# Keys of a head pair split once and carried over by DMAs, with 10 plain float32 heads instead of 12

## The chip, the cores and the metric

One core of one Trainium2 chip. The metric is the device time of one execution in microseconds (us), the median of several runs. A profiled execution has a time of its own, which is named where it is used.

## The reference

Three layers follow one another on 4 batches of 448 rows and 768 columns, all float32. The first is attention with 12 heads of 64 columns, where a sigmoid stands in place of a softmax:

```python
scores = scale * np.matmul(q, k.transpose(0, 1, 3, 2)) - np.log(S)
attn = 1.0 / (1.0 + np.exp(-scores))
return np.matmul(attn, v).astype(np.float32)
```

The second mixes each row with the row before it by two learned vectors (`mu_k`, `mu_r`), and computes sigmoid(xr @ w_r) * (relu(xk @ w_k)^2 @ w_v). The third is a mixer: a token part, u = x + relu(xt @ w_tok1) @ w_tok2, and a channel part, u + relu(u @ w_ch1) @ w_ch2. The matrices of weights arrive as float64 and are narrowed in the kernel.

## The kernel before, in words

Products of float32 accuracy are made from the fast type float32r. `split` (line 97) rounds an operand to float32r (the high part, a cast on ScalarE or VectorE, by the table of line 38) and subtracts that from the operand (the low part, always VectorE). A product then takes the high parts and the cross terms as separate matmuls.

Attention works by pairs of heads, six pairs a batch. `unit_k` (line 161) splits the keys of one head. The scores contract over 64 columns only, so the tile K has the high part of a head's keys in the half of the partitions that is the head's own, and the low part in the other half, and one matmul takes both. The keys of a pair arrive as one tile `kn`, head 0 in partitions 0 to 63 and head 1 in 64 to 127; two such tiles are held, and once both heads are split, `load_k` fetches the pair two further on. `unit_q` (line 172) splits the queries, doubled over both halves of the partitions, and the values. `unit_qk` (line 191) makes half of the scores of a head, takes the sigmoid on ScalarE, and rounds and subtracts again (lines 211 to 218). `unit_av` (line 221) multiplies with the values.

A head in the set `NATIVE` (line 51) is plain in its second product: neither its values nor its sigmoids are split, and `unit_av` makes 4 plain float32 matmuls (line 230), of which the trace records two passes each, and one copy out of PSUM. Any other head takes 7 float32r matmuls (lines 235 and 237), a copy of one half of the result on ScalarE (line 239) and an add on VectorE (line 240). Of batch 0, heads 1 to 7 and 11 are plain; of batch 1, heads 1, 4, 8 and 9; of batches 2 and 3 none.

`attention_units` (line 242) writes these units in one order. For batch 0 they run at the start, with the two mixings of each pair's columns behind it; after unit number `TOK2` the token weights are loaded and narrowed, and after number `EARLY` the first chunk of weights is made ready. The attention of each later batch is spread evenly over the matmuls of the batch before (lines 594 and 609 to 615). `first_part` (line 431) makes the second layer and the token part of one batch, `second_part` (line 532) the channel part of two batches. The weights come in chunks. At their first use a chunk is loaded as 768 KB of float64 into one of two `raw` tiles, narrowed by ScalarE and VectorE (line 268), stored as float32 for later use, and split; later uses load the stored copy.

SP issues every DMA, in order. A scheduler turns the written order into one order for each engine's queue; each queue then runs in that order and waits on semaphores. The temporaries of the pool `tmps` have four buffers of one tag, shared by the mixings and the second layer.

Of the kernel before, what the change touches and what calls it, by code (L numbers as in the profile page):

```python
# [9 lines left out]
F32 = mybir.dt.float32  # L10
F32R = mybir.dt.float32r
U32 = mybir.dt.uint32
BF16 = mybir.dt.bfloat16
# [4 lines left out]
B, H, S, D = 4, 12, 448, 64  # L18
# [4 lines left out]
P = 128  # L23
NT = C // P
NPAIR = H // 2
# [8 lines left out]
def f32(ap):  # L34
    return ap.bitcast(F32)


ONDVE = [('K', 0), ('K', 1), ('K', 2), ('K', 3), ('Q', 0), ('Q', 2), ('Q', 3), ('V', 1), ('V', 2), ('kk', 0), ('kk', 3), ('mix', 1), ('mix', 2), ('mix', 3), ('prev', 2), ('sq', 2)]

# [2 lines left out]
END_1 = 1.0  # L42
BEG_2 = 0.15
END_2 = 0.65
EARLY = 20
TOK2 = 20

NATIVE = {(0, 1), (0, 7), (0, 4), (1, 1), (0, 3), (1, 8), (1, 4), (0, 6), (0, 2), (0, 5), (1, 9), (0, 11)}


def native(b, pr, h):
    return (b, 2 * pr + h) in NATIVE


@with_exitstack
def kernel(
# [21 lines left out]
    PE, ACT, DVE, POOL, SP = nc.tensor, nc.scalar, nc.vector, nc.gpsimd, nc.sync  # L81

    def pool(name, bufs, **kw):
        return ctx.enter_context(tc.tile_pool(name=name, bufs=bufs, **kw))

    const, big = pool("const", 1), pool("big", 1)
    wraw, wpool, wsplit = pool("wraw", 2), pool("wpool", 2), pool("wsplit", 3)
    dram = pool("dram", 1, space=bass.MemoryType.DRAM)
    tmps = pool("tmps", 4)
    a1, a2, a3 = pool("a1", 1), pool("a2", 2), pool("a3", 3)  # L90
    ps_mm = pool("ps_mm", 3, space=PSUM)
    ps_av, ps_sc = pool("ps_av", 1, space=PSUM), pool("ps_sc", 2, space=PSUM)

    def ENG(kind, b):
        return DVE if (kind, b) in ONDVE else ACT

    def split(hi, lo, src, engine):
        if engine is ACT:
            ACT.copy(hi, src)  # L99
        else:  # L100
            DVE.tensor_copy(hi, src)
        DVE.tensor_tensor(out=lo, in0=src, in1=f32(hi), op=ALU.subtract)  # L102
# [4 lines left out]
    kns, qns, vns = {}, {}, {}  # L107

    def load_k(g):
        if g < B * NPAIR:  # L110
            kns[g] = a2.tile([P, 4 * P], F32, tag="kn", name="kn")
            SP.dma_start(out=kns[g], in_=k[g])

    def load_q(g):
        if g < B * H:
            qns[g] = a3.tile([P, S], F32, tag="qn", name="qn")
            SP.dma_start(out=qns[g], in_=q[g])

    def load_v(g):
        if g < B * NPAIR:  # L120
            vns[g] = a2.tile([P, 2, 4, D], F32, tag="vn", name="vn")
            SP.dma_start(out=vns[g], in_=v[g])
# [3 lines left out]
    DVE.memset(warm, 0.0)  # L126
    ACT.activation(warm, warm, AF.Sigmoid)

    zero = const.tile([P, S], BF16, tag="zero", name="zero")
    POOL.memset(zero, 0.0)  # L130
    idle = ps_av.tile([P, 512], F32, tag="av", name="idle")
    for _ in range(WARM):
# [25 lines left out]

    att = {}

    def unit_k(b, pr, h):
        g = b * NPAIR + pr
        kn = kns[g]
        me = slice(h * D, h * D + D)
        ot = slice(D - h * D, P - h * D)
        K = a3.tile([P, 4 * P], F32R, tag="KK", name="KK")
        split(K[me], K[ot], kn[me], ENG("K", b))
        att[(b, pr, h)] = {"K": K}
        if h == 1:
            load_k(g + 2)  # L170

    def unit_q(b, pr, h):
        g = b * NPAIR + pr
        st = att[(b, pr, h)]
        qn = qns.pop(2 * g + h)
        Q1 = a2.tile([P, S], F32R, tag="Q1", name="Q1")
        Q2 = a2.tile([P, S], F32R, tag="Q2", name="Q2")
        split(Q1, Q2, qn, ENG("Q", b))
        st["Q"] = (Q1, Q2)
        load_q(2 * g + h + 3)  # L180
        vn = vns[g][:, h]
        if native(b, pr, h):
            st["v"] = vn
        else:
            vs = a3.tile([P, 4, 2 * D], F32R, tag="vs", name="vs")
            split(vs[:, :, 0:D], vs[:, :, D:], vn, ENG("V", b))
            st["v"] = vs
        if h == 1:
            load_v(g + 2)

    def unit_qk(b, pr, h, c2):
        st = att[(b, pr, h)]
        K, (Q1, Q2) = st["K"], st["Q"]
        ps = ps_sc.tile([P, 2, 512], F32, tag="sc", name="psc")
        for j in range(2):
            c = c2 * 2 + j
            PE.matmul(ps[:, j, :S], K[:, c * P : (c + 1) * P], Q1, start=True, stop=False)  # L197
            PE.matmul(ps[:, j, :S], K[:, c * P : (c + 1) * P], Q2, start=False, stop=True)  # L198
        plain = native(b, pr, h)
# [21 lines left out]
    def unit_av(b, pr, h):  # L221
        st = att.pop((b, pr, h))
        vs = st["v"]
        ps = ps_av.tile([P, 512], F32, tag="av", name="pav")
        me = slice(h * D, h * D + D)
        ot = slice(D - h * D, P - h * D)
        if native(b, pr, h):
            for c in range(4):
                n = P if c < 3 else TAIL
                PE.matmul(ps[:D, :S], vs[:n, c], st[c // 2][:n, c % 2], start=(c == 0), stop=(c == 3))  # L230
            ACT.copy(xe[me, pr, 1:], ps[:D, :S])
            return
        for c in range(4):
            ah, al = st[c // 2]
            PE.matmul(ps[:, :S], vs[:, c], ah[:, c % 2], start=(c == 0), stop=(c == 3))  # L235
            if c < 3:
                PE.matmul(ps[:, :S], vs[:, c], al[:, c % 2], start=False, stop=False)  # L237
        tmp = a1.tile([P, S], F32, tag="avt", name="avt")
        ACT.copy(tmp[me], ps[ot, :S])
        DVE.tensor_tensor(out=xe[me, pr, 1:], in0=ps[me, :S], in1=tmp[me], op=ALU.add)  # L240

    def attention_units(b, then=()):

        u = [lambda: unit_k(b, 0, 0), lambda: unit_q(b, 0, 0), lambda: unit_k(b, 0, 1)]
        for pr in range(NPAIR):
            nx = pr + 1 < NPAIR
            u.append(lambda pr=pr: unit_qk(b, pr, 0, 0))
            u.append(lambda pr=pr: unit_q(b, pr, 1))
            if pr:
                u.append(lambda pr=pr: unit_av(b, pr - 1, 1))  # L250
                u += [f[pr - 1] for f in then]
            u.append(lambda pr=pr: unit_qk(b, pr, 0, 1))
            if nx:
                u.append(lambda pr=pr: unit_k(b, pr + 1, 0))
            u.append(lambda pr=pr: unit_qk(b, pr, 1, 0))
            u.append(lambda pr=pr: unit_av(b, pr, 0))
            if nx:
                u.append(lambda pr=pr: unit_q(b, pr + 1, 0))
                u.append(lambda pr=pr: unit_k(b, pr + 1, 1))
            u.append(lambda pr=pr: unit_qk(b, pr, 1, 1))  # L260
        u.append(lambda: unit_av(b, NPAIR - 1, 1))
        u += [f[NPAIR - 1] for f in then]
        return u
# [317 lines left out]
    for i, unit in enumerate(attention_units(0, [mix_units("r", box, 0), mix_units("k", box, 0)])):  # L581
        unit()
        if i == TOK2:
            load_tok2()
            w_raw(1)
        if i == EARLY:
            w_ready(1)
# [10 lines left out]
    rows, u = [], []  # L598
# [104 lines left out]
```

## Time and profile before

| what | value |
|---|---|
| median of 3 runs | 938.99 us (938.84 to 939.93) |
| profiled execution, its own time | 939.26 us |
| its span, first to last instruction | 937.5 us |
| TensorE busy | 925.3 us, 4472 matmuls |
| VectorE busy | 660.1 us |
| ScalarE busy | 516.7 us |
| DMA | 137.38 MB, 147 GB/s over the span |

The engines are named PE (TensorE matmul), PEld (TensorE weight load, which overlaps PE), DVE (VectorE), ACT (ScalarE), POOL (GpSimd) and SP (SyncE). Matmuls are pipelined: a record's duration reaches into the next record, so the time of a block of matmuls is read from start to start. Tensor names are the program's: `KK` are the split keys, `kn` the keys as loaded, `psc` the scores in PSUM, `pav` the product with the values, `al` and `ah` the parts of the sigmoids, `vs` the split values, `whi` and `wlo` the split weights. The granted clock of TensorE is 1.00 of full speed throughout.

### The profile page before, as it was taken

To read this page: it belongs to the slowest core of one execution; us is meant where nothing else is said; L and a number is where in the kernel's file an instruction comes from. 1 tells how busy PE (TensorE), PEld (TensorE's weight loads), DVE (VectorE), ACT (ScalarE), POOL (GpSimd) and SP (SyncE) were. 2 spreads that over 40 slices of the span, in tenths; PEclk is the share of its full clock that TensorE was granted. 3 is DMA by queue.
4 is the path that set the end of the run, shared out by engine and by line. 5 is a ranking of instruction groups with operands and counts; after the bars stand their busy time and mean duration, and the time that the engine had idled before them with its cause. 6 is when DMAs were issued, how large, how long until landed. Compare 5 with 4: busy or idle time off the path is not lost.

```text
span 937.5 us, 12121 instructions
## 1 busy us (share of the span) xinstructions
PE 925.3 (99%) x4472; PEld 804.4 (86%) x4472; DVE 660.1 (70%) x1111; ACT 516.7 (55%) x794; POOL 1.3 (0%) x10
## 2 busy tenths in 40 slices
PE   8999999999999999999999999999999999999998
PEld 4476778778998989889898999999999999898987
DVE  8999899989567898777879479988745552332231
ACT  6998989674674757555641367767444342112210
POOL 0000000000000000000000000000000000000000
PEclk9999999999999999999999999999999999999999
DMA  7637765765444456475444343323335321242132
GB/s 235 225 132 223 248 223 193 230 231 162 122 137 131 143 194 229 155 223 192 163 143 156 130 133 107 111 66 104 102 111 154 112 80 51 81 133 73 51 99 74
DMA packets 57084, 137.38 MB, mean 147 GB/s; under 512 B 6593, under 2 KB 23489, under 8 KB 57025
## 3 DMA queue, kind: packets, MB, share of 16 engines
q1 hardware_dynamic: 57024, 136.61, 45.4%
q8 instruction: 35, 0.57, 0.3%
q14 instruction: 25, 0.20, 0.1%
HBM read 106.96 MB, written 29.62 MB: 146 GB/s over the span
## 4 chain that ended last, share of the span: by engine, by line
PE 88%; DVE 6%; ACT 3%; DMA 2%; issue 1%; ACTq 0%; SPq 0%; DVEq 0%
PE psmm L415 25%; PE psmm L412 24%; PE psmm L414 24%; PE pav L230 3%; PE psc L197 3%; PE psc L198 3%; PE pav L235 2%; PE pav L237 2%; DMA raw<-in_moe_w_k_dram 2%; PE psmm L465 1%; DVE wlo L102 1%; DVE wd L278 1%; ACT a L204 1%; DVE wd L281 1%; DVE KK L102 1%
## 5 line engine op out<-in xcount | busy, mean ns | idle before, releaser
L412 PE MATMUL psmm<-Ah,whi 128*128 128x448 f32 (+2 forms) x688 | 249.1, 363 | 2.7 <-ACT whi L99 2.7
L415 PE MATMUL psmm<-Ah,wlo 128*128 128x448 f32 (+2 forms) x688 | 249.3, 362 | 0.8 <-DVE wlo L102 0.6
L99 ACT CAST whi<-wd 128x768 fp32r<-128x768 f32 (+1 forms) x160 | 121.4, 760 | 229.6 <-PE psmm L414 209.8
L414 PE MATMUL psmm<-Al,whi 128*128 128x448 f32 (+2 forms) x672 | 243.4, 362 | 0.1
L102 DVE TENSOR_TENSOR wlo<-wd,whi 128x768 fp32r<-128x768 f32 (+1 forms) x160 | 137.6, 861 | 97.6 <-ACT whi L99 96.0
L412 PE MATMUL psmm<-Mh,whi 128*128 128x448 f32 (+2 forms) x480 | 176.2, 367 | 0.1
L415 PE MATMUL psmm<-Mh,wlo 128*128 128x448 f32 (+2 forms) x480 | 175.6, 366 | 0.1
L414 PE MATMUL psmm<-Ml,whi 128*128 128x448 f32 (+2 forms) x480 | 174.7, 364 | 0.0
L412 PEld LDWEIGHTS psmm<-Ah,whi 128*128 128x128 f32 x688 | 129.1, 188 | 18.4 <-ACT whi L99 3.7
L415 PEld LDWEIGHTS psmm<-Ah,wlo 128*128 128x128 f32 x688 | 129.2, 188 | 13.7 <-DVE wlo L102 2.3
L414 PEld LDWEIGHTS psmm<-Al,whi 128*128 128x128 f32 x672 | 126.2, 188 | 11.7 <-DVE Al L102 0.6
L204 ACT ACTIVATE a<-psc 128x896 f32<-128x896 f32 x96 | 86.9, 914 | 29.8 <-PE psc L198 29.6
L415 PEld LDWEIGHTS psmm<-Mh,wlo 128*128 128x128 f32 x480 | 90.1, 188 | 11.7 <-DVE wlo L102 1.5
L412 PEld LDWEIGHTS psmm<-Mh,whi 128*128 128x128 f32 x480 | 90.2, 188 | 10.5 <-issue 0.7
L414 PEld LDWEIGHTS psmm<-Ml,whi 128*128 128x128 f32 x480 | 90.2, 188 | 8.5
L197 PE MATMUL psc<-Q,KK 128*128 128x448 f32 x192 | 71.5, 373 | 0.5 <-ACT a L204 0.4
L198 PE MATMUL psc<-Q,KK 128*128 128x448 f32 x192 | 70.3, 367 | 0.7 <-DVE Q L102 0.7
L211 ACT CAST ah<-a 128x896 fp32r<-128x896 f32 x72 | 67.7, 943 | 1.0
L273 ACT ACTIVATE wd<-raw 128x768 f32<-128x768 f32 (+2 forms) x54 | 45.1, 835 | 26.0 <-DVE wlo L102 11.4
L278 DVE SCALAR_TENSOR_TENSOR wd<-wd,raw 128x768 uint32<-128x768 uint32 (+2 forms) x54 | 47.1, 874 | 14.0 <-ACT wd L273 9.0
L235 PE MATMUL pav<-ah,vs 128*128 128x448 f32 x144 | 53.3, 370 | 0.2 <-DVE ah L218 0.2
L275 ACT ACTIVATE raw<-raw 128x768 uint32<-128x768 uint32 (+2 forms) x54 | 45.3, 838 | 9.4 <-DMA raw<-in_moe_w_ch_dram 8.4
(81 smaller groups left out, 1035.4 us busy)
## 6 DMA issues: line engine op xcount, KB each, us to landing
wd<-w SPq DMA_DIRECT2D x66, 384.0 KB, 3.1
raw<-in_moe_w_ch_dram SPq DMA_DIRECT2D x24, 768.0 KB, 4.8
w<-wd SPq DMA_DIRECT2D x38, 384.0 KB, 2.7
qn<-in_q_dram SPq DMA_DIRECT2D x48, 224.0 KB, 2.8
wd<-w SPq DMA_DIRECT2D x42, 256.0 KB, 2.7
kn<-in_k_dram SPq DMA_DIRECT2D x24, 256.0 KB, 2.7
vn<-in_v_dram SPq DMA_DIRECT2D x24, 256.0 KB, 3.2
raw<-in_moe_w_k_dram SPq DMA_DIRECT2D x8, 768.0 KB, 6.1
```

What stands on the lines that cost most here:

```text
L99: ACT.copy(hi, src)
L102: DVE.tensor_tensor(out=lo, in0=src, in1=f32(hi), op=ALU.subtract)
L197: PE.matmul(ps[:, j, :S], K[:, c * P : (c + 1) * P], Q1, start=True, stop=False)
L198: PE.matmul(ps[:, j, :S], K[:, c * P : (c + 1) * P], Q2, start=False, stop=True)
L204: ACT.activation(a, ps[:, :, :S], AF.Sigmoid, bias=-math.log(S), scale=1.0 / math.sqrt(D))
L211: ACT.copy(ah, a)
L235: PE.matmul(ps[:, :S], vs[:, c], ah[:, c % 2], start=(c == 0), stop=(c == 3))
L275: ACT.activation(lo, lo, AF.Copy, bias=0.4375, scale=0.875 * 2.0**-29)
L278: DVE.scalar_tensor_tensor(out=dst, in0=dst, scalar=3, in1=lo, op0=ALU.logical_shift_left, op1=ALU.bitwise_or)
L412: PE.matmul(ps[:, :n], wh, xh, start=(i == 0), stop=False)
L414: PE.matmul(ps[:, :n], wh, xl, start=False, stop=False)
L415: PE.matmul(ps[:, :n], wl, xh, start=False, stop=(i == count - 1))
```

## The change

The keys of a pair are now one unit, `unit_k(b, pr)`. For the first pair of a batch it splits the two heads as before, both ahead of the first query. For every other pair it rounds all 128 partitions at once into the K tile of head 1, subtracts in place in `kn`, and two DMAs carry the two halves of head 0's K: the high part from the K tile of head 1, the low part from `kn`. A third DMA, in the later unit `unit_k2`, writes head 1's low part over the half that head 0's high part has left; the load of the keys two pairs on follows it. `unit_k` stands earlier in the order of units, ahead of the other product of the pair before. Heads 1 and 11 of batch 0 leave the set of plain heads. The K tiles have four buffers instead of three; to make room, the zero tile and the copy of line 239 move to the pool `tmps`. `EARLY` and `TOK2` go from 20 to 18, one unit earlier in the new order.

```diff
-EARLY = 20
-TOK2 = 20
+EARLY = 18
+TOK2 = 18
...
-NATIVE = {(0, 1), (0, 7), (0, 4), (1, 1), (0, 3), (1, 8), (1, 4), (0, 6), (0, 2), (0, 5), (1, 9), (0, 11)}
+NATIVE = {(0, 7), (0, 4), (1, 1), (0, 3), (1, 8), (1, 4), (0, 6), (0, 2), (0, 5), (1, 9)}
...
-    a1, a2, a3 = pool("a1", 1), pool("a2", 2), pool("a3", 3)
+    a2, a3, a4 = pool("a2", 2), pool("a3", 3), pool("a4", 4)
...
-    zero = const.tile([P, S], BF16, tag="zero", name="zero")
+    zero = tmps.tile([P, S], F32, tag="tmp", name="zero").bitcast(BF16)[:, :S]
...
-    def unit_k(b, pr, h):
+    def unit_k(b, pr):
         g = b * NPAIR + pr
         kn = kns[g]
-        me = slice(h * D, h * D + D)
-        ot = slice(D - h * D, P - h * D)
-        K = a3.tile([P, 4 * P], F32R, tag="KK", name="KK")
-        split(K[me], K[ot], kn[me], ENG("K", b))
-        att[(b, pr, h)] = {"K": K}
-        if h == 1:
+        K = [a4.tile([P, 4 * P], F32R, tag="KK", name="KK") for _ in range(2)]
+        halves = [(slice(h * D, h * D + D), slice(D - h * D, P - h * D)) for h in range(2)]
+        if pr == 0:
+            for h, (me, ot) in enumerate(halves):
+                split(K[h][me], K[h][ot], kn[me], ENG("K", b))
+        else:
+
+            (me, ot), mine = halves[0], K[1]
+            split(mine, kn.bitcast(F32R), kn, ENG("K", b))
+            SP.dma_start(out=f32(K[0][me]), in_=f32(mine[me]))
+            SP.dma_start(out=f32(K[0][ot]), in_=kn[me])
+        for h in range(2):
+            att[(b, pr, h)] = {"K": K[h]}
+        if pr == 0:
             load_k(g + 2)
+
+    def unit_k2(b, pr):
+        g = b * NPAIR + pr
+        SP.dma_start(out=f32(att[(b, pr, 1)]["K"][:D]), in_=kns[g][D:])
+        load_k(g + 2)
...
-        tmp = a1.tile([P, S], F32, tag="avt", name="avt")
+        tmp = tmps.tile([P, S], F32, tag="tmp", name="avt")
...
-        u = [lambda: unit_k(b, 0, 0), lambda: unit_q(b, 0, 0), lambda: unit_k(b, 0, 1)]
+        u = [lambda: unit_k(b, 0), lambda: unit_q(b, 0, 0)]
...
             u.append(lambda pr=pr: unit_q(b, pr, 1))
+            if nx:
+                u.append(lambda pr=pr: unit_k(b, pr + 1))
             if pr:
...
-            if nx:
-                u.append(lambda pr=pr: unit_k(b, pr + 1, 0))
...
-                u.append(lambda pr=pr: unit_k(b, pr + 1, 1))
+                u.append(lambda pr=pr: unit_k2(b, pr + 1))
```

## Rows read from the trace of the kernel before

**Rows 1.** The page, busy us (share of the span) and instructions of TensorE.

```profile
PE 925.3 (99%) x4472; PEld 804.4 (86%) x4472; DVE 660.1 (70%) x1111; ACT 516.7 (55%) x794; POOL 1.3 (0%) x10
```

**Rows 2.** The waits of TensorE: who waited for whom, us, times, longest.

```profile
PE psmm L412 <- ACT whi L99: 2.7, 2, 1.5
```

**Rows 3.** Busy us of each engine by stretch (length, PE, PEld, DVE, ACT, POOL, clock, DMA).

```profile
15.00:45.00 30.00, 29.98 (x92) 13.22 (x93) 27.96 (x49) 26.55 (x41) 0.00 (x0) 1.00 0.74 237
45.00:90.00 45.00, 44.79 (x191) 32.79 (x190) 44.19 (x73) 43.55 (x66) 0.00 (x0) 1.00 0.51 159
90.00:135.00 45.00, 41.55 (x182) 32.13 (x181) 39.79 (x63) 36.64 (x55) 0.00 (x0) 1.00 0.68 233
135.00:215.00 80.00, 79.44 (x373) 64.06 (x372) 74.77 (x135) 61.84 (x104) 0.00 (x0) 1.00 0.69 227
215.00:937.50 722.50, 717.89 (x3599) 655.16 (x3597) 462.15 (x772) 339.74 (x521) 0.00 (x0) 1.00 0.40 126
```

**Rows 4.** TensorE's timeline (start, length) around a plain and a split head.

```profile
19.27 3.36 PE L230 MATMUL pav<-a,vn 128*64 128x448 f32 x8
...
22.56 0.47 PE L197 MATMUL psc<-Q,KK 128*128 128x448 f32 x1
...
301.24 0.37 PE L235 MATMUL pav<-ah,vs 128*128 128x448 f32 x1
...
302.66 0.60 PE L465 MATMUL psmm<-ident,r 128*128 128x128 f32 x4
```

**Rows 5.** Groups by shape (busy us, mean ns): what a split head adds.

```profile
L102 DVE TENSOR_TENSOR vs<-vn,vs 128x256 fp32r<-128x256 f32 x36 | 15.1, 419 | 0.5
...
L215 DVE TENSOR_TENSOR al<-a,ah 128x896 fp32r<-128x896 f32 x36 | 39.2, 1089 | 13.7 <-ACT ah L211 13.5
...
L217 DVE TENSOR_TENSOR al<-a,ah 128x448 fp32r<-128x448 f32 x36 | 22.4, 622 | 2.7 <-ACT ah L211 2.2
...
L218 DVE TENSOR_TENSOR ah<-a,ah 64x448 fp32r<-64x448 f32 x36 | 22.4, 623 | 1.0
...
L240 DVE TENSOR_TENSOR xe<-pav,avt 64x448 f32<-64x448 f32 x36 | 22.3, 621 | 6.2 <-ACT avt L239 5.6
...
L211 ACT CAST ah<-a 128x896 fp32r<-128x896 f32 x72 | 67.7, 943 | 1.0
...
L99 ACT CAST vs<-vn 128x256 fp32r<-128x256 f32 x16 | 6.4, 405 | 3.7 <-DMA vn<-in_v_dram 3.6
```

**Rows 6.** The same view: the two key steps, and a subtract of 128 partitions.

```profile
L101 DVE CAST KK<-kn 64x512 fp32r<-64x512 f32 x48 | 20.1, 418 | 3.2 <-DMA kn<-in_k_dram 2.6
...
L102 DVE TENSOR_TENSOR KK<-kn,KK 64x512 fp32r<-64x512 f32 x48 | 33.0, 686 | 1.5
...
L102 DVE TENSOR_TENSOR wlo<-wd,whi 128x512 fp32r<-128x512 f32 x56 | 38.4, 687 | 21.3 <-ACT whi L99 21.2
```

**Rows 7.** Timeline of the start: VectorE's key steps, TensorE's first reading of pair 1.

```profile
3.43 0.87 DVE L101 CAST KK<-kn 64x512 fp32r<-64x512 f32 x2 [2.57 <-DMA kn<-in_k_dram]
...
8.35 0.68 DVE L102 TENSOR_TENSOR KK<-kn,KK 64x512 fp32r<-64x512 f32 x1
...
12.90 0.37 PE L197 MATMUL psc<-Q,KK 128*128 128x448 f32 x1
```

**Rows 8.** DMA issues (KB, us to landing), and two raw loads on SP's timeline.

```profile
kn<-in_k_dram SPq DMA_DIRECT2D x24, 256.0 KB, 2.7
...
86.77 0.38 SPq L308 DMA_DIRECT2D raw<-in_moe_w_k_dram  x1
...
98.52 0.37 SPq L308 DMA_DIRECT2D raw<-in_moe_w_k_dram  x1
```

**Rows 9.** Groups by shape: weight loads of a plain and of a split head.

```profile
L235 PEld LDWEIGHTS pav<-ah,vs 128*128 128x128 f32 x144 | 27.0, 188 | 4.4 <-DVE ah L218 1.4 <-DVE xe L240 0.3
...
L230 PEld LDWEIGHTS pav<-a,vn 128*64 128x64 f32 x72 | 8.4, 136 | 14.3 <-issue 11.4 <-ACT xe L231 1.3 <-DVE xe L240 0.8
```

## The prediction

> **What bounds the kernel now.** I read the page first. TensorE is busy 925.3 of 937.5 us and its weight loads 804.4 us [rows 1]. Busy time overlaps from matmul to matmul, so the second reading is what TensorE waits for by name: the longest of these waits in the whole run, for the rounded weights of ScalarE, sums to 2.7 us [rows 2]. Third, the span cut into stretches [rows 3]. From 215 us on TensorE is busy 717.9 of 722.5 us while VectorE needs 462 and ScalarE 340: there nothing but fewer matmuls can shorten the run. Between 15 and 215 us the three engines are nearly level. From 15 to 45 us TensorE is busy 29.98 of 30, ScalarE 26.55, VectorE 27.96. From 45 to 90 us it is 44.79, 43.55 and 44.19 of 45: whoever gets more work there becomes the bound. From 90 to 135 us TensorE loses 3.45 us, the most of any stretch, while VectorE and ScalarE idle 5.2 and 8.4 us; something else is late there, the raw weights (below). So the reader should see a matmul-bound run with a fifth at the front where VectorE and ScalarE are level with TensorE, and the change works mostly in that fifth.
>
> **Two heads from plain float32 to split.** A plain head's attention times values is eight passes; one such block runs from 19.27 to 22.56 us, where the next matmul starts: 3.29 us. A split head's seven matmuls start at 301.24 us and the next kind at 302.66: 1.42 us [rows 4]. Each head moved saves TensorE 1.87 us, two save 3.7. Start to start is the price here, not the recorded duration, since records overlap. The Trainium skill (Perfetto Trace Analysis, Identifying the Most-Contended Engine) says that matmul busy time misleads and that the weight loads' busy share is to be read. On that measure eight loads of 136 ns (1.09 us) give way to seven of 188 ns (1.32 us) [rows 9], so the two heads would cost TensorE 0.5 us instead of saving 3.7. The start times of rows 4 decide for me, and the other reading is a rival below.
>
> What the two heads add [rows 5]: on VectorE the subtract of the values 0.42, the wide subtract 1.09, the two narrow ones 0.62 each and the final add 0.62, 3.37 us a head; on ScalarE two rounding copies of 0.943 and the rounding of the values 0.405, 2.29 us a head (the copy out of PSUM stands in either version). Both heads are of batch 0: VectorE +6.7 us, ScalarE +4.6 us, the first head at 10 to 20 us, the second (head 11) in the stretch of 45 to 90 us.
>
> **Keys of a pair at once.** For each pair but the first of a batch, two casts of 64 partitions (0.418 us) and two subtracts (0.686 us) become one of each over 128 partitions. A subtract of 128 x 512 takes 0.687 us [rows 6], so partitions cost nothing; the 128 x 512 cast is not in the trace, and I take the 64 x 512 one's price, with that of two as the other end. Saved: 1.10 us a pair, 5.5 us a batch, 22 us of VectorE in all; if the cast is no faster, 0.69 a pair. In batch 0 this leaves VectorE 6.7 - 5.5 = +1.2 us; in batch 1 it has 5.5 us less. The 11 us of batches 2 and 3 lie after 215 us beside a full TensorE: nothing.
>
> **What each part gives.** Head 1 sits in the stretch where TensorE alone is full. ScalarE has 3.45 us free there for 2.3 more, VectorE 2.0 us free plus 3.3 us from three pairs of keys for 3.4 more. I count the full -1.9 us (ends 0 and -1.9). Head 11 sits in the level stretch: ScalarE gets 2.3 us more and has 1.45 us free, so TensorE's 1.9 us is handed back as waits for the rounding copy. I count 0; ends -1.9 (ScalarE's work slides behind 90 us, where it idles 8.4 us) and +0.9 (2.3 - 1.45). The relief of VectorE in batch 1 can win back at most what TensorE loses from 90 to 215 us, 3.45 + 0.56 = 4.0 us [rows 3]. Most of that is late raw weights, which VectorE's relief doesn't hurry, so I take -1.0, near the end of the second stretch, with ends 0 and -4.0.
>
> **The three transfers a pair.** Each is 128 KB from SBUF to SBUF on SP's queue. No such transfer is in the trace; the nearest row is the key load, 256 KB from HBM, 2.7 us [rows 8]. Below nothing they can't go, as nobody got keys by a transfer before. The keys of pair 1 of batch 0 are subtracted at 8.35 us (done at 9.04) and first read at 12.90 [rows 7]: 3.9 us for a path that now needs 2.7 us and the issue. The change also cuts these keys earlier in the order. So 0 to 2.7 us once, and I take 0.5. The third transfer overwrites what the first reads and so waits for its landing, and behind it in SP's order wait the load of the keys two pairs on and whatever comes next, raw weights among them. In batches 1 to 3 the two-pair lead of that key load covers a late start; if it were gone, VectorE's next cast would wait 2.7 us. Moving head 1's keys ahead of the first query: both casts already run back to back at 3.43 us [rows 7], so one subtract of 0.69 us can come ahead of the query, and VectorE does the same work before the first full score; 0, ends 0 and 0.7. The copy buffer that moves into the shared temporaries, the zero tile and the earlier placing of the token weights and the first weight chunk (one unit earlier) I cost at nothing: a buffer of that pool is held for about one copy and one add, and there are four.
>
> **Sum.** -1.9 (head 1) + 0 (head 11) - 1.0 (VectorE's relief) + 0.5 (transfers) = -2.4 us against the profiled execution, 939.26 us (span 937.5 and 1.8 around it). The median, 938.99, lies 0.3 below it: 936.6 us. About 0.2%, 1.9 us, is what a measurement of this kernel tells from no change; 937.1 is the bound.
>
> **Rivals.** *TensorE is the bound throughout.* For it: busy 44.79 of 45 even in the level stretch, and only 2.7 us in its longest sum of waits. Then both heads pay in full, -3.7, and the relief gives -2.0 of its 4.0: 938.99 - 5.7 = 933.3 us. Against: ScalarE at 97% from 45 to 90 us is given 2.3 us more. Chance 0.24.
>
> *The front is bound by ScalarE and VectorE, and TensorE's saving goes.* For it: the level stretch, and VectorE's +1.2 us in batch 0. Both heads give 0, relief -1.0, transfers +0.5: 938.5 us, no change. The Trainium skill's weight-load measure above, taken alone, ends here too, +0.5 for the heads and 939.0 in all; the trace speaks against its reason and not against its result. Chance 0.22, of which the weight-load reading has 0.02.
>
> *Slower: the transfers stand in front of the raw weights.* The raw weights of the first use have two buffers; a refill of one buffer starts at 86.77 and its next at 98.52 us, 11.8 us apart [rows 8], and from 90 to 135 us this loop is what TensorE's 3.45 us are lost to. SP issues in order. If the third transfer of a pair waits for the first's landing with a raw load behind it, that load starts 2.7 us late. Three pairs of batch 1 are prepared between 77 and 135 us; with two of them in the way, +5.4 us, less the 2.4 gained, +3.0: 942.0 us, and 941.0 where the other buffer hides 1.0 us of it. It decides where SP reaches the third transfer before the first has landed. Against: that transfer is written two units later, so in most pairs the first has long landed. By the Trainium skill (SBUF — State Buffer, "Can I just issue two DMAs to hit both halves?") transfers to the two partition halves do not run side by side; the two for head 0 would then take 5.4 us, by rows 8, an estimate, and pair 1 would be 1.5 us late rather than 0.5. No row here shows a 64-partition transfer. Chance 0.19.
>
> That the change fails to do what it says I leave out: rows 6 show the price of 128 partitions outright.
>
> **How the numbers follow.** The forecast has 0.35, its own range 935 to 938: 0.29 of it faster, 0.06 within the bound. The full gain adds 0.24 to faster. The lost saving adds 0.22 to no change. The slower case gives 0.17 to slower and 0.02 to no change. Faster 0.53, same 0.30, slower 0.17. The range reaches from 932.0 (the full gain of 933.3 with another third of the 4.0 us won back; all of it would be 931.3) to 941.0 (the milder form of the slower case).
>
> **What would show it.** In the new profile TensorE has 16 plain passes fewer and 14 split matmuls more, and the blocks keep 3.29 and 1.42 us. Key subtracts number 28 instead of 48 (8 of the first pairs, 20 wide ones of about 0.69 us); VectorE falls by about 15 us in all. Right: at equal places in the matmul order TensorE is some 2 us ahead by 45 us, no further ahead at 90, a little more by 215, and unchanged after. Wrong on head 11: the lead grows between 45 and 90 us. Wrong on the transfers: TensorE's weight loads for scores wait on key transfers in batch 0, or raw loads start more than 12 us apart from 87 to 135 us. Wrong altogether if the time differs after 215 us by more than it did there.

## The result, and the profile after

The changed kernel takes 945.15 us (median of 4 runs, 943.14 to 945.51) against 939.2 us for the kernel before, run beside it: a ratio of 1.0062 with a 95% interval of 1.0048 to 1.0076. It is 5.8 us slower. The forecast was 936.6 us and faster; the time lies outside its range. The execution profiled took 944.95 us (span 943.2).

The page of the changed kernel, the lines that answer to [rows 1] (busy us, share of the span, instructions), then the end of its chain of waits:

```profile
span 943.2 us, 12216 instructions
PE 924.5 (98%) x4470; PEld 804.6 (85%) x4470; DVE 642.7 (68%) x1081; ACT 521.4 (55%) x800; POOL 1.3 (0%) x10
PE 77%; DVE 8%; DMA 8%; ACT 4%; issue 2%; SPq 0%; ACTq 0%; DVEq 0%
```

TensorE's busy time fell by only 0.8 us while the span grew by 5.7, so TensorE stands idle more. VectorE fell by 17.4 us, and the kernel is slower all the same: its busy total is not what counts. DMAs now make 8% of the chain; before they made 2% (TensorE 88, VectorE 6, ScalarE 3).

The stretches that answer to [rows 3] (length; PE, PEld, DVE, ACT, POOL busy; clock, DMA share, GB/s):

```profile
15.00:45.00 30.00, 28.11 (x90) 13.18 (x90) 26.49 (x48) 26.42 (x41) 0.00 (x0) 1.00 0.76 235
45.00:90.00 45.00, 40.88 (x177) 30.89 (x177) 42.21 (x71) 43.03 (x64) 0.00 (x0) 1.00 0.60 195
90.00:135.00 45.00, 42.87 (x187) 32.71 (x185) 38.90 (x60) 37.58 (x55) 0.00 (x0) 1.00 0.80 262
135.00:215.00 80.00, 77.31 (x362) 62.10 (x362) 71.52 (x126) 63.64 (x108) 0.00 (x0) 1.00 0.70 227
```

From 15 to 45 us TensorE lost 1.9 us of busy time, from 45 to 90 us 3.9, and there all three engines are less busy than before: TensorE 40.88, VectorE 42.21, ScalarE 43.03 of 45. No engine is full. They wait for one another, in the stretch where [rows 3] showed three level engines.

TensorE's waits of the changed kernel from 60 to 90 us (who waited for whom, us, times, longest); the kernel before has no row in this stretch:

```profile
PE psc L212 <- ACT a L219: 1.4, 1, 1.4
PE pav L250 <- DVE xe L255: 1.2, 1, 1.2
PE psmm L430 <- DVE wlo L102: 0.8, 1, 0.8
PE psmm L427 <- ACT Ah L99: 0.4, 1, 0.4
PE psmm L429 <- DVE Al L102: 0.3, 1, 0.3
```

Five short waits for five different things: scores wait for a score buffer that ScalarE's sigmoid frees, a product for the one product buffer that VectorE's add frees, the rest for mixed columns and weights. No key is among them. This is the end of batch 0, where head 11 is.

Where the lag stops is seen at equal places in the work. The last subtract of the weights of the first use, the 28th chunk (start and length of a row of two, of which it is the first), in the kernel before and then in the changed one:

```profile
200.10 1.55 DVE L102 TENSOR_TENSOR wlo<-wd,whi 128x512 fp32r<-128x512 f32 x2
```

```profile
205.77 1.55 DVE L102 TENSOR_TENSOR wlo<-wd,whi 128x512 fp32r<-128x512 f32 x2
```

It is 5.7 us late, and 5.7 us is the difference of the spans. By this mark the loss lies before 206 us. I summed TensorE's idle time against each matmul's own pitch (0.203 us from start to start for 448 split columns, 0.411 for a plain pass): the changed kernel has some 9 us more of it. Less the 3.7 that the two heads save, that gives 5 to 6 us. The largest pieces are 75 to 90 us (0.6 before, 4.3 after) and the first 30 us (about 2 more). Where the lag that stays comes in is seen by counting TensorE's matmuls from the end, so that both kernels have the same number left: the changed one is 0.9 us behind at 55 us, 2.9 at 79, 3.7 at 102, 2.5 at 127 and 5.9 at 193 in the executions profiled. So more than half of it comes in behind batch 0's attention, between 127 and 193 us. In one execution of the version without transfers told below, it grows there from 1.3 to 4.9 us too.

The price of the blocks and of the keys, in TensorE's timeline and VectorE's groups by shape, for [rows 4 and 6]:

```profile
21.50 3.36 PE L245 MATMUL pav<-a,vn 128*64 128x448 f32 x8
...
24.79 0.47 PE L212 MATMUL psc<-Q,KK 128*128 128x448 f32 x1
```

```profile
L101 DVE CAST KK<-kn 128x512 fp32r<-128x512 f32 x20 | 8.4, 421 | 0.0
...
L102 DVE TENSOR_TENSOR kn<-kn,KK 128x512 fp32r<-128x512 f32 x20 | 13.7, 686 | 0.1
...
L102 DVE TENSOR_TENSOR KK<-kn,KK 64x512 fp32r<-64x512 f32 x8 | 5.5, 687 | 0.3
```

A plain block is 3.29 us as before, and a cast of 128 partitions takes no longer than one of 64. The transfers, from the DMA issues (count, KB, median us from issue to landing), for [rows 8]:

```profile
kn<-in_k_dram SPq DMA_DIRECT2D x24, 256.0 KB, 3.0
KK<-kn SPq DMA_DIRECT2D x40, 128.0 KB, 3.6
KK<-KK SPq DMA_DIRECT2D x20, 128.0 KB, 3.4
```

By the medians, half the bytes of a key load, moved inside SBUF, land later than the load from HBM. And SP, the engine that issues nearly every load, now waits for them (SP's waits, whole run):

```profile
SPq L112 <- DMA KK<-kn: 23.2, 8, 6.2
SPq L184 <- DMA KK<-KK: 20.5, 11, 5.5
SPq L175 <- PE psc L213: 18.6, 9, 4.6
```

Line 112 is the key load two pairs on, which overwrites the tile that the last transfer reads and so waits for its landing; line 184 is the third transfer. In the first 60 us these two waits make 5.9 and 1.7 us. Raw weights stand behind them. The sixth raw load of the run, on SP's timeline before, after, and in the version with the same ten plain heads and without transfers:

```profile
39.15 0.41 SPq L308 DMA_DIRECT2D raw<-in_moe_w_r_dram  x1
```

```profile
50.55 0.42 SPq L323 DMA_DIRECT2D raw<-in_moe_w_r_dram  x1
```

```profile
50.65 0.43 SPq L321 DMA_DIRECT2D raw<-in_moe_w_r_dram  x1
```

It is 11.4 us late after the change, and as late without a single transfer. So with ten plain heads this lateness needs no transfer.

### The profile page after: what moved, and what is told of

It reads as the page before. It is cut to its first block, busy times and chain, and to the rows that moved or that the text cites. A ratio compares the mean times of both kernels' runs of the same rounds, so it can differ in the third digit from the quotient of the medians.

```text
span 943.2 us, 12216 instructions
## 1 busy us (share of the span) xinstructions
PE 924.5 (98%) x4470; PEld 804.6 (85%) x4470; DVE 642.7 (68%) x1081; ACT 521.4 (55%) x800; POOL 1.3 (0%) x10
## 4 chain that ended last, share of the span: by engine, by line
PE 77%; DVE 8%; DMA 8%; ACT 4%; issue 2%; SPq 0%; ACTq 0%; DVEq 0%
PE psmm L430 22%; PE psmm L427 22%; PE psmm L429 22%; DMA raw<-in_moe_w_ch_dram 3%; PE psc L212 3%; PE psc L213 3%; PE pav L250 2%; PE pav L252 2%; DMA raw<-in_moe_w_r_dram 1%; PE pav L245 1%; DVE wd L293 1%; DMA raw<-in_moe_w_k_dram 1%; DMA raw<-in_moe_w_v_dram 1%; DVE wd L296 1%; DVE Al L102 1%
## 5 line engine op out<-in xcount | busy, mean ns | idle before, releaser
L226 ACT CAST ah<-a 128x896 fp32r<-128x896 f32 x76 | 71.5, 943 | 1.2
L250 PE MATMUL pav<-ah,vs 128*128 128x448 f32 x152 | 56.6, 373 | 1.4 <-DVE xe L255 1.2
```

Of the source, the lines that this page charges most:

```text
L226: ACT.copy(ah, a)
```

## The experiments

Three questions: which part loses the time, what about that part costs it, and what of the two heads' saving is real. Single executions of one kernel lie mostly within 2 to 4 us of its median, one lies 7 us above it, so the verdicts go by the ratio of several runs to the kernel before on the same chip, with its 95% interval. Profiles say where.

### The parts one by one

**The change without the two heads.** The changed kernel with the 12 plain heads of before:

```diff
-NATIVE = {(0, 7), (0, 4), ..., (1, 9)}
+NATIVE = {(0, 1), (0, 7), (0, 4), ..., (1, 9), (0, 11)}
```

> The changed kernel with the 12 plain heads of before; transfers, order and buffers as changed. Theory 'heads' (the two heads' extra ScalarE and VectorE work in batch 0 costs more than TensorE's 3.7 us): back to 939 or less. Theory 'transfers' (key transfers delay keys and the DMAs behind them): 945 or more, since TensorE gets 3.7 us back on top. Theory 'order' (the new order and placing of the units): 945 or more as well.

942.1 us, 1.0032 (1.0020 to 1.0043): in none of the three ranges.

**The two heads without the rest.** The kernel before with two entries less:

```diff
-NATIVE = {(0, 1), (0, 7), (0, 4), ..., (1, 9), (0, 11)}
+NATIVE = {(0, 7), (0, 4), ..., (1, 9)}
```

> The kernel before with only the 10 plain heads. Theory 'heads': 943 to 945. Theories 'transfers' and 'order': between 935.5 (the full 3.7 us) and 939.

941.77 us, 1.0035 (1.0021 to 1.0050), where the kernel before took 938.6 beside it. So both halves lose, 0.32% and 0.35%. Together they would make about the 0.62% of the whole, but the next runs show that the parts don't simply add. The heads, which I had counted as the gain, cost 3.2 us.

**The change without the transfers.** All pairs split half by half at the new place in the order, ten plain heads:

```diff
-        if pr == 0:
+        if True:
             for h, (me, ot) in enumerate(halves):
...
-        if pr == 0:
-            load_k(g + 2)
+        load_k(g + 2)
```

> The changed kernel with every pair's keys split directly, head by head, in the changed place and order: no transfers, 22 us of VectorE work back. 10 plain heads, buffers as changed. Theory 'transfers': 935 to 939. Theory 'heads': 943 to 947. Theory 'order': 945 or so.

946.05 us, 1.0075 (1.0060 to 1.0090). With ten plain heads the transfers and the relief that they bring to VectorE together make no measurable difference: the interval overlaps that of the change.

**The earlier placing.** The changed kernel with its two placing constants at 19, half way back to 20:

```diff
-EARLY = 18
-TOK2 = 18
+EARLY = 19
+TOK2 = 19
```

> The changed kernel with EARLY and TOK2 at 19, so that the token weights and the first chunk come behind the same unit as before. If the earlier placing is the cause: 941 or less. Theories 'heads' and 'transfers': 945, within 1.5.

943.92 us, 1.0055 (1.0036 to 1.0074): not to be told from the change.

**The order alone.** The edit of the third run and the 12 plain heads: new order, new buffers, no transfers, no moved heads.

```diff
-NATIVE = {(0, 7), (0, 4), ..., (1, 9)}
+NATIVE = {(0, 1), (0, 7), (0, 4), ..., (1, 9), (0, 11)}
...
-        if pr == 0:
+        if True:
...
-        SP.dma_start(out=f32(att[(b, pr, 1)]["K"][:D]), in_=kns[g][D:])
-        load_k(g + 2)
+        pass
```

> The changed kernel with 12 plain heads and every pair's keys split directly, without transfers: what is left is the order of the units, the placing and the buffers. Theory 'order and buffers': 942 to 944. Theory 'transfers' (the 3.5 us that the changed kernel with 12 plain heads lost come from the transfers): 938 to 940.

938.63 us, 0.9995 (0.9986 to 1.0004). The new order costs nothing, so in the first run (1.0032) the transfers do, net of VectorE's relief. It also shows that the parts don't add: order alone -0.05% and heads alone +0.35%, but both together (the third run) +0.75%. That rest was not resolved.

**The buffers alone.** The kernel before with four key tiles and with the copy buffer and the zero tile in the shared temporaries.

```diff
-    zero = const.tile([P, S], BF16, tag="zero", name="zero")
+    zero = tmps.tile([P, S], F32, tag="tmp", name="zero").bitcast(BF16)[:, :S]
...
-        K = a3.tile([P, 4 * P], F32R, tag="KK", name="KK")
+        K = a4.tile([P, 4 * P], F32R, tag="KK", name="KK")
...
-        tmp = a1.tile([P, S], F32, tag="avt", name="avt")
+        tmp = tmps.tile([P, S], F32, tag="tmp", name="avt")
```

> The kernel before with the changed buffers alone: four key tiles, the copy of line 239 and the zero tile in the shared temporaries. If the shared temporaries hold up the copy or the mixings: 940.5 or more, with waits at line 239 or 399. If the order of the units is the cause: 938 to 939.5.

937.15 us, 0.9989 (0.9974 to 1.0004): nothing, as the prediction had it.

### The two heads

**One head at a time.** The kernel before, first with (0, 1) alone moved to split, then with (0, 11) alone.

```diff
-NATIVE = {(0, 1), (0, 7), (0, 4), ..., (1, 9), (0, 11)}
+NATIVE = {(0, 7), (0, 4), ..., (1, 9), (0, 11)}
```

```diff
-NATIVE = {(0, 1), (0, 7), (0, 4), ..., (1, 9), (0, 11)}
+NATIVE = {(0, 1), (0, 7), (0, 4), ..., (1, 9)}
```

> The kernel before with head 1 of batch 0 alone moved to split (11 plain heads). The ten plain heads alone measured 3.2 us over before. Theory 'start' (VectorE is full from 5.5 to 15 us, so head 1's extra work delays the start): +1.5 to +3, and head 11 little. Theory 'level stretch' (head 11's extra ScalarE and VectorE work and the two-step emptying of the one product buffer hit the stretch of 45 to 90 us): within 1 us of before, or 1 to 2 us faster.

> The kernel before with head 11 of batch 0 alone moved to split (11 plain heads). Theory 'level stretch': +1.5 to +4, with TensorE's losses rising between 60 and 90 us. Theory 'start': within 1 us of before, or up to 1.9 us faster.

1.0000 (0.9983 to 1.0017) and 1.0005 (0.9992 to 1.0018). Either head alone is free within its interval and shows no gain; together they cost 0.35%. That fits a slack that one head uses up. In the profile with both heads moved, TensorE waits in the same stretch as in the changed kernel, 60 to 90 us:

```profile
PE psmm L412 <- ACT Ah L99: 1.0, 2, 0.8
PE psc L198 <- DVE Q L102: 0.9, 1, 0.9
PE pav L235 <- DVE xe L240: 0.7, 1, 0.7
PE psc L197 <- DVE KK L102: 0.3, 1, 0.3
PE psmm L414 <- DVE Al L102: 0.3, 1, 0.3
```

These waits are not the loss by themselves. Head 11 alone loses as much to the pitch there in its profile (7.3 us; both heads 7.1, before 2.1), then loses some 4 us less than before from 90 to 135 us, and costs nothing.

**Is it ScalarE?** The prediction priced head 11 by ScalarE's free time. So in the changed kernel the rounding of batch 0's mixed columns goes from ScalarE to VectorE:

```diff
-ONDVE = [..., ('kk', 3), ('mix', 1), ...]
+ONDVE = [..., ('kk', 3), ('mix', 0), ('mix', 1), ...]
```

> The changed kernel (10 plain heads) with batch 0's rounding of the mixed columns on VectorE: 12 copies of 0.56 us leave ScalarE, 12 of 0.39 us come to VectorE. Theory 'ScalarE is the bound of the front' (the two heads' 4.6 us of ScalarE work is what costs): 939 to 942. Theory 'chains and buffers' (waits from one unit to the next, not an engine's load): 944 to 947.

951.25 us, 1.0126 (1.0109 to 1.0143). Both theories are missed, upwards. If ScalarE alone were the bound this would have helped; it cost 6 us more. VectorE has no room for it either.

**Other heads.** The changed kernel with heads 8 and 9 of batch 1 moved in place of 1 and 11 of batch 0.

```diff
-NATIVE = {..., (1, 1), (0, 3), (1, 8), (1, 4), ..., (1, 9)}
+NATIVE = {(0, 1), ..., (1, 1), (0, 3), (1, 4), ..., (0, 11)}
```

> The changed kernel with 10 plain heads, but the two that move to split are heads 8 and 9 of batch 1 instead of 1 and 11 of batch 0. Theory 'level front' (batch 0 has no room on ScalarE and VectorE, batch 1's later part has): 938 to 941, that is the 942.1 of the 12 plain heads less up to 3.7. Theory 'the plain heads cost nothing where they are' (any two heads moved lose): 944 to 946.

943.29 us, 1.0046 (1.0029 to 1.0062), against 1.0032 for the changed kernel with no head moved. The result lies between the two ranges: two split heads of batch 1 bring no gain either.

**Less preparation.** If the heads' extra work hurts only because it pushes back the splitting of weights, which VectorE does between the attention steps, a lighter preparation should give the time back. The last of the steps that turn raw weights into float32 is left out, the one that puts in the sign (so these weights lose their signs), in the kernel before, in the one with ten plain heads, and in the changed one:

```diff
-        DVE.scalar_tensor_tensor(
-            out=dst, in0=hi, scalar=0x80000000, in1=dst, op0=ALU.bitwise_and, op1=ALU.bitwise_or
-        )
```

> The kernel before without the last step of the narrowing of the weights (the step that puts the sign in, so the weights lose their signs): 54 instructions of 0.69 to 0.95 us leave VectorE, some 46 us, all of them before 490 us. Theory 'preparation' (the preparation of the weights on VectorE and ScalarE sets the pace to about 200 us): 925 to 934. Theory 'TensorE is the bound': within 2 us of before.

> The same cut in the kernel with only the 10 plain heads (3.2 us over before with the full narrowing). Theory 'preparation': TensorE's 3.7 us now show, so 1 to 4 us below the cut kernel before. Theory 'chains of the two heads' (waits inside the heads, whatever VectorE's load): 2 to 4 us above it.

> The changed kernel without the last step of the narrowing (the weights lose their signs). Theory 'preparation': level with the cut kernel before or up to 4 us below it, where the full one was 6 above. Theory 'order and transfers for themselves': 3 to 6 us above it.

0.9978 (0.9965 to 0.9991), 0.9993 (0.9982 to 1.0003) and 1.0018 (1.0004 to 1.0032). The first takes 935.85 us. Its VectorE is busy 38.1 us less in the profile (622.0 against 660.1), the 28th chunk is ready 10.6 us earlier, and only 2.1 us are gained, so the preparation does not set the pace of the run: both theories' ranges are missed, the second barely. Between the cut kernels the heads cost 0.15% where they cost 0.35%, and the whole change 0.40% where it cost 0.62%. By the middle values some 2 us of either loss go with the preparation, but with 0.10 to 0.15% of uncertainty in each ratio neither is told from nothing. The waits at the end of batch 0 stay: in the one execution profiled with ten plain heads and the cut, the sum against the pitch shows 6.7 us lost from 60 to 90 us (2.1 in the cut kernel before).

**The heads' saving without their work.** The decisive run. The kernel before with (0, 1) and (0, 11) split, but their sigmoids are written rounded in one instruction and have no low parts (the high part stands in for them). The 14 matmuls remain; of the work of [rows 5] the ScalarE rounding copies, 3.8 us for both heads, and VectorE's subtracts of the sigmoids, 4.7 us, are gone.

```diff
+        if b == 0 and 2 * pr + h in (1, 11):
+            ah = a3.tile([P, 2, S], F32R, tag="ah", name="ah")
+            ACT.activation(ah, ps[:, :, :S], AF.Sigmoid, ...)
+            st[c2] = (ah, ah)
+            return
```

> The kernel before with 10 plain heads, where the sigmoids of heads 1 and 11 of batch 0 are written rounded and their low parts left out (the high part is multiplied twice): TensorE does the same matmuls as with split heads, ScalarE loses the four copies (3.8 us) and VectorE the subtracts (4.7 us). Theory 'extra work' (the two heads' ScalarE and VectorE work is what costs, and TensorE's saving counts once it is gone): 934.5 to 936.5. Theory 'pace' (the front's pace is set on ScalarE and VectorE, so TensorE's 3.7 us show nowhere): level with before, within 1 us, and the waits between 60 and 90 us stay above those of before.

935.41 us, 0.9973 (0.9962 to 0.9985). Now the two heads gain 2.5 us of the 3.7. TensorE's saving is real, and the work left out is worth 0.62%, 5.8 us. The engines from 45 to 90 and from 90 to 135 us (the columns of the stretches above) with ten plain heads, and then from 45 to 90 us with the light ones:

```profile
45.00:90.00 45.00, 41.73 (x173) 31.48 (x172) 44.07 (x72) 41.59 (x62) 0.00 (x0) 0.96 0.49 162
90.00:135.00 45.00, 44.58 (x195) 34.27 (x194) 43.46 (x69) 39.52 (x57) 0.00 (x0) 1.00 0.75 252
```

```profile
45.00:90.00 45.00, 43.03 (x187) 32.80 (x187) 43.89 (x72) 41.29 (x63) 0.00 (x0) 1.00 0.54 173
```

TensorE does 14 matmuls more in the same 45 us (the lower clock of the first execution took 1.4 us of it, see the end), and VectorE and ScalarE show nearly the same busy time as with the full heads: the time freed was filled by other work. VectorE is the full engine here, 98% busy in both, and with the full heads from 90 to 135 us as well (43.46 of 45, where [rows 3] have 39.79): the heads push its other work back. The 28th chunk is ready at 198.4 us with the light heads and at 202.4 with ten plain heads (200.8 before). The run leaves out load and, with it, two steps of the chain from the sigmoid to the product; which of the two cost the time it doesn't tell.

### The transfers

**Idle transfers.** The new order without moved heads (0.9995 above), and beside it three transfers of 128 KB a pair that write a spare tile which nobody reads. The spare tile's own write order makes SP wait at times, as the changed kernel's transfers do; the DMA scratch is smaller, 256 for 1024, to make room, here and in the next two runs.

```diff
+        if pr:
+            SP.dma_start(out=spare[:D], in_=f32(K[1][:D]))
+            SP.dma_start(out=spare[D:], in_=f32(K[0][D:]))
+        load_k(g + 2)
...
+        SP.dma_start(out=spare[:D], in_=f32(att[(b, pr, 1)]["K"][D:]))
```

> 12 plain heads, the changed order, keys split directly (938.6), and three transfers a pair at the places of the real ones, of the same size, into a spare tile that nobody reads. Theory 'traffic': 941 to 943. Theory 'hold': 938 to 939.5, since no raw key tile and no reader waits for them.

940.37 us, 1.0022 (1.0003 to 1.0040), between the two ranges. Nobody waits for these keys, and by the middle value most of the 0.32% is there.

**A sixteenth of the bytes.** The same with 32 of the 512 columns.

```diff
-            SP.dma_start(out=spare[:D], in_=f32(K[1][:D]))
+            SP.dma_start(out=spare[:D, :32], in_=f32(K[1][:D, :32]))
```

> The idle transfers again (three a pair into a spare tile that nobody reads, keys split directly, 12 plain heads), at the same places of SP's queue and with the same waits, but a sixteenth of the bytes. The full ones measured 1.0022 of before, the same kernel without them 0.9995. Theory 'bytes': back to 0.999 to 1.000. Theory 'SP's order' (the places and waits in the queue hold the raw weights up): 1.002 to 1.003, with the sixth raw load again later than 45 us.

939.56 us, 1.0012 (1.0000 to 1.0024): between nothing and the full transfers, and its interval overlaps both neighbours. The sixth raw load starts at 44.2 us here, at 37.2 with the order alone and at 52.5 with the full idle transfers, so of its lateness about half goes with the places and half with the bytes. That doesn't price them: with head 1 alone moved it starts at 45.4 us and costs nothing. Whether bytes or places in SP's queue cost the time is not settled.

**A third tile for the raw keys.** In the changed kernel with 12 plain heads VectorE waits once, long, for a key load held up behind a transfer (VectorE's timeline, the bracket is the wait):

```profile
15.45 0.62 DVE L102 TENSOR_TENSOR Q<-qn,Q 128x448 fp32r<-128x448 f32 x1
19.99 0.43 DVE L101 CAST KK<-kn 128x512 fp32r<-128x512 f32 x1 [3.91 <-DMA kn<-in_k_dram]
```

With three raw key tiles in place of two that load need not wait:

```diff
-            kns[g] = a2.tile([P, 4 * P], F32, tag="kn", name="kn")
+            kns[g] = a3.tile([P, 4 * P], F32, tag="kn", name="kn")
```

> The changed kernel with 12 plain heads (942.1) and three raw key tiles instead of two. Theory 'hold': the raw tile is now held until the third transfer has landed, so the load of the keys two pairs on starts at 15.7 us instead of 10.8 and VectorE stands 3.9 us at the start of batch 0; with a third tile that wait goes and the time is 938 to 939.5. Theory 'traffic' (the transfers' bytes and places in SP's queue): 942, within 1.

943.05 us, 1.0042 (1.0026 to 1.0058). The wait is gone; that cast now follows within the run of VectorE's steps:

```profile
15.75 0.42 DVE L101 CAST KK<-kn 128x512 fp32r<-128x512 f32 x1
16.09 0.62 DVE L102 TENSOR_TENSOR Q<-qn,Q 128x448 fp32r<-128x448 f32 x1
16.62 0.68 DVE L102 TENSOR_TENSOR kn<-kn,KK 128x512 fp32r<-128x512 f32 x1
20.30 0.68 DVE L417 SCALAR_TENSOR_TENSOR mix<-xe,mur,mix 128x448 f32<-128x448 f32 x1 [2.99 <-ACT mix L414]
```

But VectorE then stands idle 3.0 us behind its next step, and the time stayed. The longest wait on an engine was not the loss: it sat in front of idle time.

**Another queue.** The changed kernel with 12 plain heads, the three transfers issued by GpSimd:

```diff
-            SP.dma_start(out=f32(K[0][me]), in_=f32(mine[me]))
+            POOL.dma_start(out=f32(K[0][me]), in_=f32(mine[me]))
```

> The changed kernel with 12 plain heads (942.1, 1.0032 of before) with its three transfers a pair issued from GpSimd's queue instead of SP's. Theory 'SP's order' (the transfers stand in SP's queue before the raw weights and the key loads, and hold them up): 937 to 940. Theory 'bytes' (the DMA engines' extra load): 941 to 943.5. The label is of another plan; the kernel is the one told here.

951.39 us, 1.0142 (1.0125 to 1.0159), far slower than either theory had it. A median landing is longer too (3.9 to 4.0 us), and the granted clock fell for a while, so it doesn't separate SP's order from the bytes.

What the transfers do to the front shows in the stretch from 15 to 45 us, first with the new order alone, then with the transfers, 12 plain heads in both:

```profile
15.00:45.00 30.00, 28.30 (x87) 12.10 (x86) 28.76 (x50) 26.05 (x40) 0.00 (x0) 1.00 0.70 234
```

```profile
15.00:45.00 30.00, 29.69 (x91) 13.00 (x91) 22.33 (x42) 24.78 (x40) 0.00 (x0) 1.00 0.82 254
```

VectorE is relieved by 6.4 us, more than the 3.3 us that three pairs of keys are worth, so it seems to do less weight work as well: the DMA share is up from 0.70 to 0.82, and the sixth raw load starts at 54.1 us, not 37.2 as with the order alone. The relief has come as idle time; that it is for want of raw weights fits these starts and is not shown further.

## Why the prediction was wrong

**What bounds the kernel.** Right in its first half: after 215 us the lag at equal places moves by about 1 us only, and VectorE's relief in batches 2 and 3 gave nothing. Right too that the change works in the first fifth and that the three engines are level from 45 to 90 us. Wrong was to price head 1 in a stretch "where TensorE alone is full": its work starts before 15 us, and from 5.5 to 15 us VectorE is busy 9.25 of 9.5 us in the kernel before and TensorE 7.41.

**The two heads.** The block prices held, 3.29 and 1.42 us. The light heads decide whether the saving is real for the start times: 935.41 us, a gain of 2.5, with the same 14 matmuls. The weight-load measure of the Trainium skill (Perfetto Trace Analysis, Identifying the Most-Contended Engine), by which these heads would cost 0.5 us of themselves, did not foretell it; the page gives that measure for how close TensorE is to its limit, not for the price of one block. The step that failed is the set of terms behind it, head 1 at a full -1.9, head 11 at 0, and their sum. I compared each head's added work with the free time in its own stretch and called it covered where it fitted; for head 11 I looked at ScalarE alone, and left VectorE out of the term, which had 3.4 us to take with 0.81 free and some relief from the keys. Measured, the two heads together give +3.2 us (1.0035) where I had -1.9, and what VectorE and ScalarE do for their sigmoids costs 5.8 us (0.9973 to 1.0035), more than the 3.7 saved. The sum of that work is 8.5 us on two engines, so some two thirds of it became time. The free time in a stretch was not free. How the work became time, as VectorE's load that pushes later work back or as longer chains in front of TensorE, the runs don't separate. The rival in which ScalarE and VectorE take the saving had the mechanism, and was sized too small: it let the saving go, while the work cost more than the saving. The lead of some 2 us that I named as a sign never came: TensorE lost about 2 us more than before by 30 us, against 1.9 saved, at equal places it is 0.9 us behind at 55 us and 2.9 at 79, and ScalarE takes the second layer's first r out of PSUM at 81.7 us (80.3 before).

**One head was no guide to two.** Head 1 alone 1.0000 (so its -1.9 did not come), head 11 alone 1.0005 (its 0 held), both 1.0035. My terms were added as if independent.

**Keys at once.** Right: 20 wide subtracts of 0.686 us and 8 narrow ones, the 128 x 512 cast 0.421 us, VectorE 17.4 us less where about 15 was forecast.

**VectorE's relief, -1.0.** Not seen. In the changed kernel the stretches from 90 us on lose as much to the pitch as before (5.5 then, 4.3 now, from 90 to 135 us; 0 and 1.8 from 135 to 150). With 12 plain heads, transfers without the relief cost 0.22% and with it 0.32%, so it doesn't show there either.

**The transfers, +0.5.** Mis-sized: with 12 plain heads they cost 0.37% against the new order alone (1.0032 and 0.9995), 3.5 us. The slower rival had transfers in front of raw weights in SP's order. With 12 plain heads raw loads do start later with transfers (the sixth at 54.1 us for 37.2), but earlier in the run than the rival looked, and in the changed kernel the sixth is as late without them. The rival's sign was no sign: its 11.8 us are two refills of one of the two buffers, and by that measure refills that start from 86 to 123 us follow 10.8 to 15.6 us apart in the kernel before and 10.5 to 13.2 in the changed one. SP's waits for landing transfers, 23.2 and 20.5 us in the whole run, are the ones the rival spoke of; what they cost no run isolates. Its other sign, TensorE waiting for keys, doesn't appear, and transfers that nobody waits for cost most of the same. My estimate of 5.4 us for the two transfers of head 0 did not come: the first two, issued at 9.71 and 10.32 us, each landed 3.44 us after its issue, both within 4.05. The Trainium skill (SBUF — State Buffer, "Can I just issue two DMAs to hit both halves?") says that transfers to the two halves serialize. These landings don't test that: a sixteenth of the bytes still takes 2.3 us in the median where the full idle transfers take 2.9, so most of a landing is not bytes, and to double a whole landing was too much.

**The price of nothing** for buffers, new order and earlier placing held: 0.9989, 0.9995 and 1.0055 beside 1.0062, none to be told from no effect. (For the new order that is so with 12 plain heads; with ten it is part of the 0.75%.)

**What is open:** bytes or queue places for the transfers; why new order and moved heads together cost 0.75% when apart they cost 0.30%; what brings in the 3.4 us of lag between 127 and 193 us; and whether the heads' work costs as load or as chain. No version tried beats the kernel before by a measurable margin with the full computation.

## What to carry to other kernels

Where three engines are level, don't call added work on a helper engine free because it fits into that engine's idle time in its stretch: two edits that are each free can cost together. Nor is a helper's work all worth the same: here 8.5 us in the heads cost 5.8, and 38 us of VectorE's preparation were worth 2.1. To see whether a saving exists at all, remove the price and keep the saving, as the light heads do. Check a sign of delay in a version without the suspect before you lay it on the suspect, as with the sixth raw load. A transfer that nobody waits for can still cost time.

## What the runs showed of the hardware that was not expected

TensorE's clock. With ten plain heads alone the granted clock was 0.96 in the mean from 45 to 90 us, and TensorE's timeline shows how, after its waits (brackets) from 63 to 67.6 us:

```profile
66.66 0.67 PE L412 MATMUL psmm<-Ah,whi 128*128 128x448 f32 x2 [0.78 <-ACT Ah L99]
67.60 0.61 PE L414 MATMUL psmm<-Al,whi 128*128 128x448 f32 x1 [0.27 <-DVE Al L102]
68.01 0.57 PE L415 MATMUL psmm<-Ah,wlo 128*128 128x448 f32 x1
68.38 0.57 PE L414 MATMUL psmm<-Al,whi 128*128 128x448 f32 x1
...
71.00 0.46 PE L235 MATMUL pav<-ah,vs 128*128 128x448 f32 x1
71.30 0.37 PE L198 MATMUL psc<-Q,KK 128*128 128x448 f32 x1
71.50 0.37 PE L197 MATMUL psc<-Q,KK 128*128 128x448 f32 x1
```

From 68.01 to 71.00 us eight matmuls start 0.374 us apart, not 0.203: the lower of the two levels, 1.2 for 2.4 GHz. That took 1.4 us in that execution. It doesn't make the loss: the four of its ten executions with a mean granted clock of 1.000 took 941.6 to 943.0 us. In the changed kernel's profile the clock stays at 1.00, though TensorE loses as much from 60 to 90 us (7.0 and 7.1 us against the pitch). With GpSimd issuing the transfers it went further, 0.89 from 15 to 45 us:

```profile
15.00:45.00 30.00, 26.38 (x70) 11.08 (x69) 18.95 (x34) 22.09 (x33) 3.62 (x7) 0.89 0.74 224
```

The other surprise is the transfer inside SBUF: 128 KB over 64 partitions takes a median of 3.4 to 3.6 us to land in the changed kernel, where 256 KB of keys from HBM take 3.0. As idle transfers, full and with a sixteenth of the bytes:

```profile
spare<-KK SPq DMA_DIRECT2D x60, 128.0 KB, 2.9
```

```profile
spare<-KK SPq DMA_DIRECT2D x60, 8.0 KB, 2.3
```
